# Spreading the Fourier transform of u over more steps of an attention loop

## The chip, the cores and the metric

The kernel runs on one core of a Trainium2 chip. The metric is the device time of one execution in microseconds, as the median of several runs. A core has five engines with a queue each: TensorE (PE, with its weight loads shown as PEld), VectorE (DVE), ScalarE (ACT), GpSimd (POOL) and SyncE (SP), which here issues all transfers between memory and the core.

## The reference

Two independent heads, whose outputs stand side by side. A is a long convolution from a state-space model: a kernel K of 2048 positions for each of 448 channels, made from 256 complex modes, is convolved with u by Fourier transforms. B is attention with 16 heads of 28 channels over 2048 positions.

```
# A: L = 2048, D = 448, N = 256
P = exp((A * dt[:, None])[:, :, None] * pos)
K = 2.0 * einsum("dn,dnl->dl", C, P).real
y = irfft(rfft(u_t, 2 * L) * rfft(K, 2 * L))[:, :, :L]
a = y.transpose(0, 2, 1) + u * D_skip
# B: H = 16, Dh = 28
q, k, v = split(x @ wqkv)
p = softmax(q @ k.T * Dh ** -0.5)
b = (p @ v).reshape(B, S, D) @ wo
out = concatenate([a, b], axis=-1)
```

## The kernel before

The program has a first part, a loop of 256 steps, and an end. All of it is written out in Python, and each engine gets its instructions in the order in which they were issued there.

The first part projects x to q, k and v, and makes the seeds of the convolution kernel, which it stores in memory. The loop does the attention: step s works on query block s // 16 (four groups of four heads, and four blocks of 512 queries in each) and on the 16th part s % 16 of the keys. While the loop runs, head A's work is done in between, by four sorts of tasks:

- *u tasks*: the transform of u. `u_stage1` has 16 jobs and `u_stage2` 16 more, of two parts each, so 64 tasks. A part does one product with a transform matrix (`mm32`, in four pieces of 32 rows, each of which the profile shows as two matmuls, so eight records), and ScalarE copies the result to a tile ub (two copies in stage 2). After the second part the result is stored, and the loads of the job after the next are issued. Inputs come in tiles ua, of which there are two.
- *k tasks*: the 56 blocks of the convolution kernel. A block begins every `KP` = 3.5 steps (`k_begin`). GpSimd then raises the powers of its e tile with nine operations (`e_power`: three sizes, three operations each), VectorE those of its g tile, and `KD` = 4 steps later PE multiplies them in three tasks, one a step: two products of e and g (`part0`), and a transform (`part1`). A block's e tile can be seeded when the products of the block before the last have been issued (`k_seed`).
- tasks at the end of a query block: `sums`, `scale` and the turning of the maxima, three in 16 steps.
- from step 192 on, the products of the spectra, the transform back, and the output (`f_slot`).

The order within a step is written out by hand in `ORDER`. For PE it is: two pairs of score products (one for the running maximum of a later block, tile pm, one for the probabilities, tile pss), a first slot, the product of probabilities and v (`pv_step`, tile po), a second slot, and two more pairs. A slot takes at most one task, in the order of `slot`: urgent ones first, then a k task that is due, then a u task that is due. The results of max products and of all tasks go through one ring of three PSUM tiles, pm.

```
ORDER = ('m0', 's0', 'm1', 's1', 'v', 'f', 'pv', 'f', 'v', 'k', 'm2', 's2', 'm3', 's3', 'v')
...
u_due = collections.deque((3 + UP * i + (UP / 2) * c + (4 if i > 15 else 0), i, c) for i in range(32) for c in range(2))
...
        elif m_due and m_due[0][0] <= s_:
            m_due.popleft()[1]()
        elif u_due and u_due[0][0] <= s_:
            u_part(*u_due.popleft()[1:])
```

After the very last u task, `load_wo` takes both ua tiles for the weights of the output projection: GpSimd clears each, and SP issues eight loads into each.

Of the kernel before, what the change touches and what calls it, by code (L numbers as in the profile page):

```python
# [39 lines left out]
UG = (2, 2, 4)  # L40
PS = 1
SGB, XB, XL = 2, 5, 4
K0, KP, KD, UP = 0, 3.5, 4, 3
A0, A1, KW = 26, 34, (33, 35, 36)

N1 = 32
# [1083 lines left out]
```

## Time and profile before

| | |
|---|---|
| median of 3 runs | 1302.44 us (1301.22 to 1304.79) |
| span of the profiled execution, first to last instruction | 1301.1 us |
| mean clock granted to TensorE in it | 0.978 |
| starts of the loop's first and last exponential | 254.7 and 1276.4 us |

The profiled execution's time is given as its span alone; no other time of it is on the page. The page gives the busy time of each engine over the span, the chain of waits that ended last, the costliest groups of instructions and the transfers; the trace behind it can be asked for any stretch. Where a row of a timeline ends in brackets, the engine sat idle before it for that time, until what stands behind the arrow was done. Nearly all instructions are recorded through one helper, so they show its line, 75, and are told apart by their tiles: out<-in.

### The profile page before, as it was taken

What the parts mean: (1) busy time and instruction counts of PE and PEld (TensorE: products, weight loads), DVE (VectorE), ACT (ScalarE), POOL (GpSimd) and SP (SyncE); (2) the same over time, 40 slices, a digit from 0 to 9 for tenths busy, and PEclk for the clock granted to TensorE, in tenths of its full rate; (3) what the DMA queues carried; (4) which work ended last, traced back from release to release, by engine and by line L of the source; (5) the groups of instructions that cost most, each with busy time, mean ns of one, the idle gap of its engine ahead of it and who ended that gap; (6) DMA issues with size and microseconds to landing.
All of it is one profiled execution on the core that took longest, in us unless ns stands there. A gap on an engine that the chain in (4) does not pass through costs nothing.

```text
span 1301.1 us, 33177 instructions
## 1 busy us (share of the span) xinstructions
PE 1228.2 (94%) x12625; PEld 701.0 (54%) x12625; DVE 948.0 (73%) x2106; ACT 952.4 (73%) x2068; POOL 871.1 (67%) x736
## 2 busy tenths in 40 slices
PE   6878985899999999999999999999999999999997
PEld 5657763355555555555555555555555555544433
DVE  5887896987777887787788888888888655645111
ACT  4775763488888888888888888888887766756552
POOL 3676683298888878888869999998996212424421
PEclk9888997999999999999999999999999999999999
DMA  6677769835866555458644131733425453647656
GB/s 194 203 258 244 249 206 294 237 77 124 195 137 149 124 146 148 140 147 231 181 126 96 54 95 32 182 91 83 103 51 148 153 158 133 201 144 244 198 162 174
DMA packets 200088, 205.35 MB, mean 158 GB/s; under 512 B 95993, under 2 KB 158521, under 8 KB 197881
## 3 DMA queue, kind: packets, MB, share of 16 engines
q1 hardware_dynamic: 199928, 203.23, 56.2%
q8 instruction: 100, 1.64, 0.5%
q14 instruction: 60, 0.48, 0.1%
HBM read 120.73 MB, written 82.18 MB: 156 GB/s over the span
## 4 chain that ended last, share of the span: by engine, by line
PE 71%; DVE 10%; DMA 6%; POOL 5%; ACT 3%; issue 3%; SPq 0%; POOLq 0%; ACTq 0%; DVEq 0%
PE pm L75 40%; PE pss L75 16%; PE po L75 15%; DVE tri L75 2%; DVE mx L75 2%; POOL e L75 1%; POOL qhat L75 1%; DMA k<-hl 1%; ACT tri L75 1%; DVE qhat L75 1%; DVE sg L75 1%; DMA tri<-in_B_wqkv 1%; DVE px L75 1%; DMA khat<-k 1%; DMA ut<-in_A_u 1%
## 5 line engine op out<-in xcount | busy, mean ns | idle before, releaser
L75 ACT ACTIVATE p<-pss 128x512 f32<-128x512 f32 x1024 | 560.9, 609 | 111.6 <-PE pss L75 108.6
L75 PE MATMUL pss<-qhat,khat 128*128 128x512 f32 x1024 | 402.5, 399 | 1.5 <-ACT p L75 1.4
L75 DVE TENSOR_REDUCE mx<-pm 128x1 f32<-128x512 f32 x500 | 321.4, 684 | 109.2 <-PE pm L75 107.1
L75 PE MATMUL pm<-khat,qhat 128*128 128x512 f32 x749 | 326.3, 438 | 3.4 <-DVE mx L75 2.1
L75 POOL TENSOR_TENSOR e<-e,sdb 128x256 f32<-128x256 f32 x168 | 202.0, 1202 | 116.2 <-ACT e L75 61.2
L75 PE MATMUL po<-p,v 128*32 128x512 f32 x2048 | 269.1, 594 | 0.0
L75 POOL TENSOR_TENSOR e<-e,eu 128x256 f32<-128x256 f32 x168 | 248.4, 1478 | 13.2
L75 PEld LDWEIGHTS pm<-khat,qhat 128*128 128x128 f32 x749 | 141.0, 189 | 199.7 <-ACT p L75 47.8
L75 DVE CUSTOM_DVE_ANT_0 rl<-pm,rl 128x512 f32<-128x512 f32 x249 | 171.4, 688 | 65.2 <-ACT rl L75 61.5
L75 PEld LDWEIGHTS pss<-qhat,khat 128*128 128x128 f32 x1024 | 190.2, 188 | 45.7 <-issue 10.8
L75 POOL TENSOR_TENSOR eu<-e,sdb 128x256 f32<-128x256 f32 x168 | 202.2, 1203 | 0.0
L75 POOL TENSOR_TENSOR p<-pr,pr 64x448 f32<-64x448 f32 x64 | 73.3, 1145 | 158.5 <-PE pm L75 133.2
L75 ACT ACTIVATE rl<-pm 128x512 f32<-128x512 f32 x249 | 150.8, 606 | 20.4 <-PE pm L75 20.4
L75 DVE TENSOR_TENSOR g<-g,zg 128x128 f32<-128x128 f32 x392 | 162.1, 413 | 3.4
L75 PE MATMUL pm<-xh,khat 112*128 112x512 f32 x256 | 94.1, 451 | 23.2 <-DVE hl L75 11.1
L75 PE MATMUL pm<-kdif,qhat 128*128 128x512 f32 x249 | 100.5, 404 | 2.6 <-DMA v<-v 1.3
L75 DVE TENSOR_TENSOR zg<-g,zg 128x128 f32<-128x128 f32 x224 | 88.0, 393 | 5.0
L75 PEld LDWEIGHTS pm<-e,g 128*32 128x32 f32 x3584 | 57.2, 109 | 43.8 <-issue 16.1
L75 DVE TENSOR_TENSOR pr<-pm,ub 128x448 f32<-128x448 f32 x64 | 37.0, 619 | 56.4 <-PE pm L75 42.0
L75 PEld LDWEIGHTS pm<-xh,khat 112*128 112x128 f32 x256 | 54.2, 217 | 39.4 <-DVE hl L75 12.9
L75 PE MATMUL pm<-e,g 128*32 128x64 f32 x3584 | 73.0, 222 | 1.9 <-POOL e L75 1.9
L75 ACT ACTIVATE y<-pm 128x448 f32<-128x448 f32 x48 | 26.5, 553 | 58.2 <-PE pm L75 33.8
(134 smaller groups left out, 1470.3 us busy)
## 6 DMA issues: line engine op xcount, KB each, us to landing
sdb<-sd SPq DMA_DIRECT2D x56, 336.0 KB
khat<-k SPq DMA_DIRECT2D x64, 256.0 KB
qhat<-q SPq DMA_DIRECT2D x64, 256.0 KB
sd<-sg SPq DMA_DIRECT2D x8, 1456.0 KB
k<-hl SPq DMA_DIRECT2D x16, 512.0 KB
q<-hl SPq DMA_DIRECT2D x16, 512.0 KB
mw<-in_mw SPq DMA_DIRECT2D x16, 512.0 KB
sd<-qhat SPq DMA_DIRECT2D x8, 896.0 KB
```

The lines of the kernel that those rows point to most:

```text
L75: i = f(*args, **kw)
```

## The change

One constant, the distance in steps from one job of the transform of u to the next. Task c of job i was due at step 3 + 3i + 1.5c and is now due at 3 + 5.5i + 2.75c, with four steps more from job 16 on in both. The last task fell in step 102 and now falls in step 181. The clearing of the ua tiles and the loads in `load_wo` move with it.

```diff
 PS = 1
 SGB, XB, XL = 2, 5, 4
-K0, KP, KD, UP = 0, 3.5, 4, 3
+K0, KP, KD, UP = 0, 3.5, 4, 5.5
 A0, A1, KW = 26, 34, (33, 35, 36)
```

## The prediction

> **What bounds the kernel now.** I read the page's table of engines first, then the busy time of each engine in stretches that hold whole steps of the loop, then the chain of waits inside a few steps, then GpSimd's timeline around the end of the transform of u.
>
> ```profile
> PE 1228.2 (94%) x12625; PEld 701.0 (54%) x12625; DVE 948.0 (73%) x2106; ACT 952.4 (73%) x2068; POOL 871.1 (67%) x736
> ```
>
> TensorE is the busiest by far, but its busy time alone doesn't say that it is the limit, so the two stages that the change touches are set side by side: the steps that carry u tasks and the steps after them that carry none. The first view counts the matmuls of `pv_step` (tile p, eight records in every step), the second the u tasks (tile ua, eight records a task), the third is of all instructions.
>
> ```profile
> core 0: us, PE busy (x) PEld busy (x) ACT busy (x), PEclk, DMA share, GB/s
> 264.30:666.30 402.00, 104.45 (x800) 20.69 (x796) 3.84 (x6) 1.00 0.60 150
> 692.90:981.10 288.20, 84.93 (x648) 16.28 (x648) 3.16 (x5) 1.00 0.37 87
> ...
> 264.30:666.30 402.00, 59.41 (x508) 15.73 (x504) 1.70 (x2) 1.00 0.60 150
> 692.90:981.10 288.20, 0.00 (x0) 0.00 (x0) 0.00 (x0) 1.00 0.37 87
> ...
> 264.30:666.30 402.00, 400.49 (x4782) 219.27 (x4778) 313.36 (x742) 335.73 (x778) 326.08 (x257) 1.00 0.60 150
> 692.90:981.10 288.20, 287.16 (x3461) 163.72 (x3453) 253.00 (x607) 244.18 (x553) 271.19 (x212) 1.00 0.37 87
> ```
>
> The first stretch is 800 / 8 = 100 steps in 402.0 us, 4.02 us a step, with 508 / 8 = 63.5 u tasks in it (the 64th lies across its edge). The second is 648 / 8 = 81 steps in 288.2 us, 3.56 us a step, without any. So the stage with the tasks pays (4.02 - 3.56) x 100 / 63.5 = 0.73 us for each. In the last two rows the columns after the length are PE, PEld, DVE, ACT and POOL. PE is busy for 99.6% in both. Beside it POOL is at 81% and 94%, DVE at 78% and 88%, ACT at 84% and 85%: the second stage is much nearer to even, and whether PE still sets its pace is the question on which the sign hangs. The chain of waits inside steps answers it. These are three neighbouring steps of the first stage:
>
> ```profile
> 604.90 0.58 PE pm L75 x32
> 605.48 0.86 PE po L75 x8
> 606.34 1.18 PE pm L75 x9
> 607.52 0.23 PE pss L75
> ...
> 609.15 0.58 PE pm L75 x32
> 609.74 0.86 PE po L75 x8
> 610.60 0.43 PE pm L75
> ...
> 613.23 0.86 PE po L75 x8
> 614.09 1.19 PE pm L75 x9
> ...
> 616.92 0.89 PE pm L75 x8
> 617.81 0.86 PE po L75 x8
> 618.67 0.43 PE pm L75
> ```
>
> A step reads: a k task in the first slot (0.58), the four `pv` products (0.86), whatever the second slot holds together with the first score product (0.43 with nothing, 1.18 with a u task), and seven more score products at 0.23. With a k task alone that is 0.58 + 0.86 + 0.43 + 7 x 0.23 = 3.48 us, and the rows agree: 609.74 to 613.23 is 3.49. With a u task as well it is 3.48 + 0.75 = 4.23; 605.48 to 609.74 is 4.26. And this is a stretch from the stage without u tasks:
>
> ```profile
> 843.12 0.86 PE po L75 x8
> ...
> 846.59 0.86 PE po L75 x8
> 847.45 0.43 PE pm L75
> ...
> 849.50 0.99 PE po L75 x8
> 850.50 0.43 PE pm L75
> ...
> 852.71 0.60 PE pm L75 x32
> 853.30 0.86 PE po L75 x8
> ```
>
> 843.12 to 846.59 is 3.47: a step with a k task takes there what it takes among u tasks, PE issuing without a break. Only the step with nothing in its slots (its `pv` starts at 849.50) is another matter: from 846.59 to 849.50 PE needs 2.91 us, and the next step, to 853.30, takes 3.80, some 0.3 us more than its work, since others fall behind there. The two steps together take 6.71, so an empty one is worth 6.71 - 3.48 = 3.23, not the 2.91 that PE needs.
>
> [...] The steps' own times, equal to the sum of PE's issue times, speak for PE.
>
> **The change part by part.** The due time of task c of job i goes from 3 + 3i + 1.5c to 3 + 5.5i + 2.75c (both with 4 more from job 16 on). The last goes from 101.5, which is step 102, to 180.25, step 181. No work is added or removed: the same 64 tasks of eight matmuls, 96 evacuations by ScalarE and the same loads and stores, in the same order among themselves. Kernel blocks keep their steps, as a k task comes before a u task in `slot`. By the due times 28 of the 64 tasks go past step 104.
>
> *Where a task lands.* Blocks start every 3.5 steps and have three k tasks each, so six of seven steps hold one. A task in such a step costs 0.75 in either stage, by the rows above. A u task in an otherwise empty step takes the first slot (0.89 at 616.92): 613.23 to 617.81 is 4.58, of which 0.75 is the task ahead of it at 614.09, so such a step takes 3.83, 0.60 more than an empty one. Going through `slot` with both sets of due times, 51 of 64 tasks share a step with a k task now, and 52 afterwards; three steps hold two u tasks and no k task now, none later. That is 1 x (0.75 - 0.60) = 0.15, and the pairs cost 0.75 for one of their two at most: I take **+0.2 us**, between -2 and +2 if the cost differs by 0.03 a task between stages.
>
> *GpSimd's wait for the last task.* `load_wo` clears the two ua buffers on POOL, behind which the powers of e wait in POOL's queue; the second clearing waits for the last u task on PE.
>
> ```profile
> 649.49 2.39 POOL L75 TENSOR_TENSOR e<-e,eu 128x1024 f32<-128x1024 f32 x1
> 652.25 0.85 POOL L75 MEMSET ua<- 128x896 f32 x1 [0.38 <-PE pm L75]
> 664.24 0.85 POOL L75 MEMSET ua<- 128x896 f32 x1 [11.14 <-PE pm L75]
> 665.05 0.63 POOL L75 TENSOR_TENSOR e<-e,sdb 128x256 f32<-128x256 f32 x1
> ...
> 670.71 1.92 POOL L75 TENSOR_TENSOR e<-e,sdb 128x1024 f32<-128x1024 f32 x1
> ...
> 674.58 2.38 POOL L75 TENSOR_TENSOR e<-e,eu 128x1024 f32<-128x1024 f32 x1
> 676.91 0.64 POOL L75 TENSOR_TENSOR e<-e,sdb 128x256 f32<-128x256 f32 x1
> ...
> 688.75 0.63 POOL L75 TENSOR_TENSOR e<-e,sdb 128x256 f32<-128x256 f32 x1
> ...
> 677.01 0.65 PE L75 MATMUL pm<-e,g 128*32 128x64 f32 x32 [0.63 <-POOL e L75]
> ...
> 688.84 0.65 PE L75 MATMUL pm<-e,g 128*32 128x64 f32 x32 [1.27 <-POOL e L75]
> ```
>
> POOL loses 11.14 us of its lead, and PE then waits 0.63 + 1.27 = 1.9 us for the next two blocks. This stall moves to step 181 and changes its shape. In the built program the clearing now stands between the sixth and the seventh of the nine operations of block 51, whose products are due in step 183; before, it stood ahead of all nine of block 29, with four steps to go. After the release POOL needs 0.81 for the clearing and 676.96 - 670.71 = 6.25 for the three large operations: block 51 is ready 7.1 us on. PE gets there in the rest of step 181 with the start of 182 (eight score products, 2.0) and step 182, which has no k task (about 3.2): 5.2. It waits 1.9. Block 52 needs a whole period, 688.75 - 676.91 = 11.84, so 18.9 us on; PE, at 7.1 plus three steps of 3.48, is there at 17.5 and waits 1.4. Block 53 is due four steps later, 13.9 against 11.84: no wait. In all 3.3 in place of 1.9, **+1.4 us**, between -1.9 (POOL far enough ahead) and +7 (below).
>
> *What is hidden.* The 16 loads of wo stand in SP's queue behind the clearing, ahead of loads of seeds for block 54 and of v for the last head group, all due five or more steps later. ScalarE's evacuations and the u loads and stores (DMA share 0.60 in the first stage, 0.37 in the second) go from the fuller to the emptier stage; no row above has PE waiting for either, so their move is worth nothing, and costs nothing as long as ACT, 85% in the second stage, stays under PE: a task costs ACT (335.73 / 100 - 244.18 / 81) x 100 / 63.5 = 0.54 us, less than the 0.75 by which it lengthens the step.
>
> Sum: 0.2 + 1.4 = +1.6 us. On the profiled execution's span of 1301.1 that gives 1302.7. The median of the runs is 1302.44, 1.3 above that span, and the forecast on it is **1304.0 us**.
>
> **The rivals.** *The second stage has room (faster).* If POOL, DVE or ACT set the pace there, PE has slack into which 28 tasks fall for less than 0.75, while the first sheds them at full price. By PE's issue times seven steps need 6 x 3.48 + 2.91 = 23.8, or 3.40 a step, against 3.56 measured, part of which are the tasks at the end of a query block. If all 0.16 over 76 steps were filled, 12 us would go: about 1292. For it speak POOL's 94% and the 0.3 us lost after an empty step; against it that the k step takes 3.47 to 3.49 in both stages, so there is nothing to fill in six steps of seven. [...]
>
> *POOL arrives late at step 181 (slower).* If POOL has not done the first six operations of block 51 when the last u task ends, they come after it. They take 670.71 - 665.05 = 5.7 us, the first wait grows to 7.5 and the second stays: 9 us in place of 1.9, with the 0.2 about 1309.7. By `k_seed` the seeds of block 51 can be written in step 177, four steps or some 14 us ahead of the release, and six operations fill 5.7 of these; it decides when POOL comes to them more than 8 us late. For it speaks POOL's 94% in the second stage, against it that with u tasks in it a block's 3.5 steps take some 13 us of PE against POOL's 11.84.
>
> *The loads of wo come in the way (slower).* If the 16 issues push a load of seeds past its use, a wait like the 1.27 above comes with each of the two to four blocks still to go: 1307 to 1309.
>
> **How the numbers follow.** About 0.3% (3.9 us) is what a measurement of this kernel can tell from no change. The forecast has 0.61, the room in the second stage 0.15, the late POOL 0.16, the loads of wo 0.08. The forecast lies within 0.3% over its own range of 1300 to 1306. The range reaches half way to the first rival, of which it leaves the rest out, and to the end of the two slower ones: 1297.0 to 1310.0. Faster by over 0.3%: 0.15; within: 0.61; slower: 0.24.
>
> **What would show it.** In the changed profile steps with a k task alone should still take 3.48 us and those with a u task 4.25, in the old second stage too; that stage, which gets 26 tasks, should grow from 3.56 to about 3.80 a step, and the first, which keeps 35, fall to about 3.81. GpSimd's wait before its second clearing should stand near step 181, with PE's two waits of 1 to 2 us for e behind it, and none near 677. Steps of the second stage that take less than 4.1 us with both tasks would prove the first rival; a wait for e over 5 us the second; waits of PE or ACT for sdb after step 181 the third.

## The result

The changed kernel takes 1308.26 us in the median of 7 runs (1306.13 to 1312.1), the kernel before 1303.8 over the 7 runs that stand beside it; the ratio is 1.0041 with a 95% interval of 1.0026 to 1.0056, about 5.3 us (the medians differ by 4.5). The profiled execution of the changed kernel has a span of 1304.4 us (its own time 1306.55), 3.3 more than before. The loop itself differs by more than that: from the first exponential to the first one of step 192 it takes 734.9 us against 729.9 before (worked out from the starts of the exponentials, four in a step). The part ahead of the loop, which is the same program, ended 2.2 us earlier in this profile; over all profiles of this study it ended between 252.5 and 257.0 us, so spans are not compared below, but the loop.

Busy time in the two stages of the prediction, 100 and 81 steps, first by the products with v (eight records a step), then for all engines (PE, PEld, DVE, ACT, POOL after the length):

```profile
261.60:644.40 382.80, 104.60 (x800) 20.58 (x800) 3.88 (x6) 1.00 0.50 120
670.10:983.70 313.60, 84.90 (x648) 16.76 (x648) 3.13 (x5) 1.00 0.48 126
```

```profile
261.60:644.40 382.80, 380.04 (x4559) 211.59 (x4555) 312.63 (x743) 319.40 (x723) 332.41 (x262) 1.00 0.50 120
670.10:983.70 313.60, 307.86 (x3677) 171.58 (x3677) 254.98 (x607) 260.36 (x608) 262.81 (x209) 1.00 0.48 126
```

The first stage falls from 4.02 to 3.83 us a step, where 3.81 was forecast. The second rises from 3.56 to 3.87, where 3.80 was forecast, and PE, busy for 99.6% of it before, is at 98.2%: it waits there for things for which it did not wait before. The waits of PE and its weight loads in the loop up to step 192, those that are new or larger (engine and tile, what it waited for, us in total, times, longest):

```profile
PEld pm L75 <- issue: 49.1, 139, 1.7
PEld pm L75 <- POOL e L75: 6.7, 10, 2.2
PE pm L75 <- POOL e L75: 3.2, 2, 1.9
PEld pss L75 <- DMA qhat<-mh: 1.6, 1, 1.6
PE pm L75 <- issue: 1.6, 1, 1.6
PE pss L75 <- DMA qhat<-mh: 1.2, 1, 1.2
```

The same rows in the list of the kernel before:

```profile
PEld pm L75 <- issue: 46.7, 140, 0.8
PEld pm L75 <- POOL e L75: 5.1, 9, 1.7
PE pm L75 <- POOL e L75: 1.9, 2, 1.3
```

Three things stand here. The wait for e was forecast; it takes 3.2 us of PE in place of 1.9. The waits of PE for the store of the maxima (qhat<-mh) and for nothing that the profile shows (issue) have no row in the kernel before. Comparing each step's length with the mean of steps of the same kind (same tasks in its slots, same neighbour) in the kernel before, the long steps are 31 and 32 (+1.5 us together), 114 (+1.9), 183 (+2.0) and 186 (+1.3) in the changed kernel, and 106 (+0.7) and 109 (+1.3) in the one before. That is 6.7 against 2.0, so 4.7 of the 5.0 us. The steps with a task of u behave as forecast: in the old second stage of the changed kernel the 18 steps with a k task and a u task take 4.25 us in the median, from one product with v to the next.

*The wait for e.* GpSimd's and TensorE's timelines around step 181:

```profile
937.41 0.84 POOL L75 MEMSET ua<- 128x896 f32 x1
947.22 0.85 POOL L75 MEMSET ua<- 128x896 f32 x1 [8.97 <-PE pm L75]
948.03 1.91 POOL L75 TENSOR_TENSOR e<-e,sdb 128x1024 f32<-128x1024 f32 x1
...
954.31 0.65 PE L75 MATMUL pm<-e,g 128*32 128x64 f32 x32 [1.90 <-POOL e L75]
957.82 0.65 PE L75 MATMUL pm<-e,g 128*32 128x64 f32 x32
966.15 0.65 PE L75 MATMUL pm<-e,g 128*32 128x64 f32 x32 [1.28 <-POOL e L75]
```

POOL had reached its first clearing at 937.41, ten microseconds ahead of the release, and PE then waits 1.90 and 1.28 us for blocks 51 and 52.

*The maxima.* The first score product of step 32, the first of query block 2, waits for the store of that block's maxima into qhat. VectorE (the first row, which makes the first of the two halves that are stored), SP's queue (start, length) and PE in the changed kernel:

```profile
361.57 0.28 DVE L75 TENSOR_SCALAR mh<-pm 16x128 fp32r<-16x128 f32 x1
...
357.81 1.84 SPq L75 DMA_DIRECT2D yu_d<-ub  x4
359.75 1.86 SPq L75 DMA_DIRECT2D ua<-in_A_u  x4
361.71 1.71 SPq L75 DMA_DIRECT2D sdb<-sd  x1
363.46 1.82 SPq L75 DMA_DIRECT2D khat<-k  x4
365.38 1.23 SPq L75 DMA_DIRECT2D qhat<-mh  x2
...
372.18 0.47 PE L75 MATMUL pss<-qhat,khat 128*128 128x512 f32 x1 [1.23 <-DMA qhat<-mh]
```

The eight transfers of a u task, a load of seeds and four loads of khat stand right ahead of the store. The first half of the maxima is ready at 361.85, but SP issues its store only at 365.38, 3.5 us later; it lands near 372, when the last row, on PE, can start. In the kernel before:

```profile
369.10 0.28 DVE L75 TENSOR_SCALAR mh<-pm 16x128 fp32r<-16x128 f32 x1
...
358.53 1.85 SPq L75 DMA_DIRECT2D yu_d<-ub  x4
...
364.82 1.82 SPq L75 DMA_DIRECT2D khat<-k  x4
369.41 1.23 SPq L75 DMA_DIRECT2D qhat<-mh  x2
```

There the transfers of a u task stand ahead of the store too, but far enough: the loads of khat are issued by 366.64, and SP issues the store at 369.41, 0.03 us after the half is ready. The next task comes in step 30, behind the store.

*A pause inside a product.* In step 114, 27 matmuls of a k task run, then nothing for 1.58 us, then the other five; no wait on any engine or transfer is recorded for it:

```profile
687.18 0.61 PE L75 MATMUL pm<-e,g 128*32 128x64 f32 x27
689.37 0.31 PE L75 MATMUL pm<-e,g 128*32 128x64 f32 x5 [1.58 <-issue]
```

```profile
676.00:680.50 4.50, 4.50 (x28) 2.24 (x28) 3.85 (x10) 4.23 (x12) 4.34 (x4) 1.00 0.86 217
680.50:684.00 3.50, 3.50 (x81) 2.27 (x80) 3.23 (x11) 3.10 (x8) 3.42 (x3) 1.00 0.89 200
```

```profile
q8 instruction: 1, 0.02, 4.1%
```

The second fence is the busy time of the engines in two stretches ahead: the DMA engines are busy for 0.86 and 0.89 (the column before the last) while the 1 MB of qhat is loaded that SP issues from 678.21 on, and then for 0.61 up to the pause. The third, of the DMA queues between 686 and 688, shows a packet of the instruction queue there; it starts at 686.72 and takes 1.31 us, so it ends 1.34 us before PE goes on. The same product in the kernel before has no pause:

```profile
708.23 0.63 PE L75 MATMUL pm<-e,g 128*32 128x64 f32 x32
```

There SP issues the four loads of qhat from 699.75 on, the DMA engines are busy for 0.90 and 0.97 from 700.0 to 704.0 and to 708.2, and a packet of the instruction queue runs from 707.36 for 1.32 us.

### The profile page after: what moved, and what is told of

It reads as the page before. It is cut to its first block, busy times and chain, and to the rows that moved or that the text cites. A ratio compares the mean times of both kernels' runs of the same rounds, so it can differ in the third digit from the quotient of the medians.

```text
span 1304.4 us, 33179 instructions
## 1 busy us (share of the span) xinstructions
PE 1227.2 (94%) x12625; PEld 699.3 (54%) x12625; DVE 948.6 (73%) x2106; ACT 952.1 (73%) x2068; POOL 869.8 (67%) x736
## 4 chain that ended last, share of the span: by engine, by line
PE 75%; DVE 10%; DMA 4%; POOL 4%; ACT 4%; issue 2%; SPq 0%; ACTq 0%; DVEq 0%; POOLq 0%
PE pm L75 42%; PE pss L75 17%; PE po L75 16%; DVE mx L75 2%; DVE tri L75 2%; POOL qhat L75 1%; ACT tri L75 1%; DVE sg L75 1%; DVE qhat L75 1%; DVE px L75 1%; DVE rl L75 1%; DMA qhat<-q 1%; DMA k<-hl 1%; POOL tri L75 1%; DVE hl L75 1%
```

## The experiments

Times are compared with runs of the kernel before on the same chip. "Loop" is the time from the first exponential to step 192, as above.

| | ratio to before, 95% interval | loop, us |
|---|---|---|
| before (profile) | 1 | 729.9 |
| changed (profile) | 1.0041, 1.0026 to 1.0056 | 734.9 |
| e1 clearing on VectorE | 1.0008, 0.9999 to 1.0018 | 731.8 |
| e2 one u task two steps later | 1.0042, 1.0027 to 1.0056 | 732.8 |
| e3 qhat loaded four steps later | 1.0016, 1.0004 to 1.0028 | 732.3 |
| e4 all u tasks 75 steps later | 0.9997, 0.9985 to 1.0008 | 730.7 |
| e5 changed kernel again | 1.0042, 1.0026 to 1.0059 | 733.7 |
| e6 load_wo five steps later | 1.0013, 0.9999 to 1.0026 | 731.6 |
| e7 e6, e2 and e3 together | 0.9983, 0.9971 to 0.9995 | 728.6 |
| e8 before, load_wo five steps later | 0.9987, 0.9975 to 0.9998 | 728.3 |

**e1, the clearing on VectorE** (in the changed kernel)

```diff
-            nc.gpsimd.memset(t, 0.0)
+            nc.vector.memset(t, 0.0)
```

> The changed kernel, with the two clearings in load_wo done by VectorE in place of GpSimd. Theory (GpSimd's queue waits for the last u task, so the powers of e come late): the steps 183 and 186, 5.32 and 4.85 us in the changed kernel, go back to 3.4 and 3.5, 3.3 us less in the loop; VectorE follows TensorE closely, so its own wait delays nothing by more than 0.5 us. Against the kernel before about +2 to +3 us in place of +5.3. Rival (those two steps are long for another reason, such as the loads of wo on SP's queue): they stay long, time as the changed kernel.

Steps 183 and 186 are back at their usual lengths, so it was the clearing in GpSimd's queue. The ratio gives +1.0 us against the kernel before (-0.1 to +2.3), less than the 2 to 3 expected. VectorE paid a little, too:

```profile
950.61 1.75 DVE L75 MEMSET ua<- 128x896 f32 x2
...
953.32 0.50 PE L75 MATMUL pm<-khat,qhat 128*128 128x512 f32 x1 [0.69 <-DVE mx L75]
```

Its two clearings hold up a reduction of maxima, and PE waits 0.69 us for it, a little over the 0.5 allowed. The wait for the maxima (0.7) and the pause (1.9) are still there.

**e2, one task behind the store of the maxima** (in the changed kernel)

```diff
-    u_due = ... + (4 if i > 15 else 0), i, c) ...
+    u_due = ... + (4 if i > 15 else 0) + (2 if (i, c) == (4, 1) else 0), i, c) ...
```

> The changed kernel, with one u task, the second part of job 4, due in step 30 in place of 28, behind the store of the maxima for query block 2. Theory (its four stores and four loads stand ahead of that store in SP's queue, together with four loads of khat): the wait of the score products for qhat<-mh near 372 us goes, steps 31 and 32 take 4.5 and 3.5 together 1.5 us less, all else as in the changed kernel. Rival (the store is late by the loads of khat alone): the wait stays within 0.3 us of its 1.6.

The wait for qhat<-mh is gone from the list of waits, and steps 31 and 32 are of usual length. SP issues the store at 365.21, as the next thing behind the loads of khat, and the task's transfers only from 370.04 on: they had made it late. The total did not fall: the ratio, 1.0042, is that of the changed kernel. Of the loop's 2.2 us less than in the changed kernel, 1.5 are this wait, but in the profile something else had come: after the wait for e in step 183, 1.89 us against 1.90 in the changed kernel, the granted clock was 0.56 for 3.9 us. Busy time around it, clock in the third column from the end:

```profile
953.70:955.60 1.90, 0.04 (x1) 0.00 (x0) 1.80 (x7) 1.43 (x3) 1.90 (x2) 1.00 0.39 100
955.60:959.50 3.90, 3.87 (x44) 1.98 (x45) 0.67 (x2) 0.22 (x1) 3.74 (x5) 0.56 0.55 146
959.50:963.00 3.50, 3.50 (x50) 2.04 (x49) 3.06 (x8) 2.98 (x8) 3.34 (x3) 1.00 0.29 104
```

A mean of 0.56 over 3.9 us is as much as half the clock for (1 - 0.56) x 3.9 / 0.5 = 3.4 us. The eight records of the products with v took 1.96 us there and 1.04 in the next step. Step 183 takes 6.9 us here, against 5.3 in the changed kernel; step 186 is of usual length, since POOL, busy for 3.74 of the 3.9 us, caught up meanwhile, and the one wait of PE without a recorded cause is 0.5 us against 1.6. On time alone e2 is inconclusive.

**e3, qhat loaded later** (in the changed kernel)

```diff
-        if kt == 2:
+        if kt == 6:
             if u + 2 < NU:
                 load_q(u + 2)
```

> The changed kernel, with the loads of the query block after the next issued in the seventh step of a block in place of the third (steps 118, 134 and so on in place of 114, 130). Theory (the pause of 1.6 us inside a product of step 114 is TensorE out of instructions, whose fetch stood behind 1 MB of loads of qhat): no pause in step 114, which takes 4.3 in place of 6.3; 1.9 us less, unless another fetch falls behind the moved loads, then one such pause at another place. Rival (the pause belongs to that place in the program whatever is loaded): step 114 stays at 6.3.

Step 114 is of usual length, and no pause over 0.5 us stands anywhere else in the loop: the list of waits has no row of PE for issue. With these loads four steps later the pause does not come; the loads alone do not make it, as the kernel before has them at the same place and no pause. That it is TensorE's instructions that come late behind them was the author's estimate: no row shows the engine waiting for instructions, and whose instructions a packet holds is not shown. The change of the loop is 2.6 us, 1.9 of it this step; the rest is the wait for the maxima, shorter in this run.

**e4, all u tasks in the second stage** (in the kernel before)

```diff
-u_due = collections.deque((3 + UP * i + ...
+u_due = collections.deque((78 + UP * i + ...
```

> The kernel before (3 steps from job to job), with all due times 75 steps later: the u tasks lie in steps 78 to 179. Theory (a task costs 0.75 us wherever there is a k task in its step): steps 3 to 77 fall to about 3.55 on average, steps 103 to 179 rise to about 4.0, the sum within 1 us of before; GpSimd's wait as before, 1.9 us in all, near step 180; in all -1 to +3 us against before, the upper end if a fetch or a store comes late somewhere. Rival (the second stage has room beside TensorE): 64 tasks there cost clearly under 0.75, 8 us or more less than before.

The same steps, 3 to 77 and 104 to 180, of e4 (first the products with v, then its u tasks) and, in the third fence, of the kernel before:

```profile
264.60:531.00 266.40, 78.65 (x600) 14.98 (x600) 2.51 (x4) 1.00 0.35 82
636.70:946.60 309.90, 80.38 (x616) 16.15 (x616) 3.15 (x5) 1.00 0.58 151
```

```profile
636.70:946.60 309.90, 44.16 (x376) 11.45 (x376) 1.69 (x2) 1.00 0.58 151
```

```profile
264.00:564.00 300.00, 78.36 (x600) 15.57 (x600) 2.50 (x4) 1.00 0.56 136
669.70:946.30 276.60, 80.70 (x616) 15.47 (x616) 3.16 (x5) 1.00 0.38 91
```

The first 75 steps lose 33.6 us, the later 77 gain 33.3 for 376 / 8 = 47 tasks, 0.71 each. So in that stage, too, a task costs about what it costs in the first, and TensorE has no room there to take it in. A pause came here too: the list of waits has one of PE for issue, of 1.2 us, ahead of a score product (pss).

**e5, the changed kernel once more**

> The changed kernel itself once more, for a second profile and more runs beside the other kernels of this set. Theory: the same four terms: score products waiting for qhat<-mh in step 31 or 32 (0.5 to 1.5 us), TensorE without instructions for 0.5 to 2 us in step 114, the waits for e in steps 183 and 186 (3.3 us), now and then half the clock for 3.4 us after one of these waits (1.7 us more); ratio 1.003 to 1.005. If the first two are chance of one run, they are missing here.

The pause is there after the same 27 matmuls, with 1.59 us, steps 183 and 186 are the same to 0.02 us, and the wait for the maxima is 0.5 us in the weight loads alone. So the pause and the waits for e belong to the program, and the maxima come at the edge: the weight loads wait 0.5 to 1.6 us for them by the run (1.1, 1.0 and 1.1 in e1, e3 and e6), and in this run no step is long for it. The lists of e1 and e6 have a wait of PE for issue as well, of 1.9 and 2.1 us. Behind the wait for e in step 183, 1.89 us, the eight records of the products with v take 1.04 us in this run, not 1.96 as in e2.

**e6, load_wo five steps after the last u task** (in the changed kernel)

```diff
         if c and i == 31:
-            load_wo()
+            wo_wait.append(5)
+
+    wo_wait = []
...
+        if wo_wait:
+            wo_wait[0] -= 1
+            if not wo_wait[0]:
+                wo_wait.clear()
+                load_wo()
         late[0] = s + NK + LEAD > NS
```

> The changed kernel, with load_wo called five steps after the last u task, so that GpSimd finds the buffers free. Theory: no wait of GpSimd on TensorE, no wait for e in steps 183 and 186, no half clock there: 3.3 us less than the changed kernel in the loop and up to 1.7 more of the clock; VectorE has no part in it, so nothing as at step 182 in the run with VectorE. Ratio to before 1.000 to 1.001. Rival (the clearing itself or the loads of wo delay the powers): waits for e of over 1 us two to four steps after the moved call.

GpSimd clears both tiles in one go, and the products of blocks 51 to 54 find their powers ready:

```profile
956.71 1.64 POOL L75 MEMSET ua<- 128x896 f32 x2
...
953.47 0.66 PE L75 MATMUL pm<-e,g 128*32 128x64 f32 x32
956.97 0.65 PE L75 MATMUL pm<-e,g 128*32 128x64 f32 x32
963.96 0.65 PE L75 MATMUL pm<-e,g 128*32 128x64 f32 x32
967.44 0.65 PE L75 MATMUL pm<-e,g 128*32 128x64 f32 x32
```

Neither the clearing itself nor the loads of wo delay anything: the list of waits has no row of PE for e or for a load of seeds. The loop is 3.3 us shorter than in the changed kernel, though its pause was longer (2.1 us against 1.6). The ratio, 1.0013, is a little over the 1.000 to 1.001 expected, well within its interval.

**e7, all three edits** (e6, e2 and e3 in the changed kernel)

> The changed kernel with all three edits: load_wo five steps later, the second part of job 4 due two steps later, the loads of qhat four steps later. Theory (nothing else is in the change): no step from 4 to 191 is over 0.45 us longer than its kind, and the loop up to step 192 takes 728 to 729.5 us, against 729.9 in the kernel before and 734.9 in the changed one; ratio to before 0.9985 to 1.000. Rival (spreading costs by itself): the loop stays above 731 us with no single long step.

No step is over 0.45 us longer than its kind. The stages:

```profile
265.30:646.50 381.20, 104.62 (x800) 20.48 (x800) 3.83 (x6) 1.00 0.51 119
672.30:981.00 308.70, 84.78 (x648) 16.64 (x648) 3.13 (x5) 1.00 0.50 128
```

3.81 us a step in both, the values that the prediction gave for a change without stalls (3.81 and 3.80). The ratio, 0.9983, is just below the range expected. Spreading by itself costs nothing that can be measured.

**e8, load_wo later in the kernel before** (the edit of e6)

> The kernel before, with load_wo called five steps after the last u task. Theory: its waits for e in steps 106 and 109 go, 1.9 us less: ratio 0.998 to 0.9995. Rival (VectorE or ScalarE hold those steps anyway): no change in them.

The waits in steps 106 and 109 are gone, 1.6 us of the loop. Beside e7's 728.6 the 728.3 of this kernel shows what the spreading of tasks costs when nothing stalls: +0.3 us, from one profile of each, and with the two other edits of e7 in it. e7 and e8 are both faster than either kernel; they differ from each other by less than the intervals can tell.

## Why the prediction was right or wrong

*What bounds the loop, and where a task lands (+0.2 us).* Right. A task costs the same in both stages: 0.73 us on average in the first stage of the kernel before, 0.71 in the second stage in e4, and the steps with both kinds of task take the 4.25 us that were forecast. The term itself is +0.3 by e7 against e8, which single profiles can't tell from nothing.

*GpSimd's wait (+1.4 us).* Right in place, form and size. Forecast were waits of 1.9 and 1.4 us for blocks 51 and 52 and none for 53; measured 1.90 and 1.28 and none. In the kernel before the two were 0.63 and 1.27. e6 shows that this, and not the clearing or the loads, is the cause.

*What is hidden (0).* Wrong, and this is the step that failed. The prediction looked for rows of the kernel before in which PE waits for u's transfers, found none, and valued their new places at nothing. It had asked which loads stand behind the clearing on SP's queue, but not what each u task's eight transfers come to stand ahead of. Those of one of the 64 now stand, with four loads of khat, so close ahead of the store of the maxima that SP issues it 3.5 us after it could: the score products behind it wait 0.5 to 1.6 us (e5 and the changed kernel), and e2 takes the wait away.

*The pause in step 114 (1.9 us)* had no term at all. What brings it is not shown: the kernel before has none, though the same 1 MB of qhat is loaded ahead of the same product (DMA engines busy for 0.97 up to it, against 0.61 in the changed kernel), e4, with the tasks moved otherwise, has one of 1.2 us, and with the loads four steps later (e3, e7) there is none.

*The sum.* +1.6 was forecast, +5.3 measured, inside the range, and the interval of 0.26% to 0.56% lies mostly beyond the 0.3% within which the likeliest case put it. That the range covers it is luck: its slower end was set by the late POOL and the loads of wo, of which neither came, and what came instead was not in the sum. The forecast terms came out at 0.3 + 1.3, the two missing ones at 1.5 + 1.9: 5.0, as the loop of the profiled run shows. In e5 the wait for the maxima cost next to nothing (loop 733.7), so 1.5 is the most that was seen of it. The lower clock of e2 (0.56 for 3.9 us) can come on top; in the stretches of the loop that are shown of the kernel before, the changed kernel, e4 and e7 the granted clock was 1.00, and how often it falls is open.

*The rivals.* Room in the second stage: refuted by e4. POOL late at step 181: it was 10 us early, even more than the 8 us of lead that the prediction reckoned with. Loads of wo in the way: no wait of that kind in any run. The time went to the slower side by two waits that were not among the rivals: the one for the maxima is of the sort of the third, a transfer that comes late, and what the other waits for no row shows.

## What to carry to other kernels

TensorE bounds this loop in both stages (busy for 99.6% of each in the kernel before), so the moved work cost nothing that could be measured: of the 5.0 us in the loop, 1.3 and 1.5 came from what it newly stood next to, and 1.9 from a pause whose cause is not shown. When tasks are moved in such a loop, list, for each engine and above all for the queue that issues the transfers, what every moved item comes to stand ahead of, and look for short deadlines there. An instruction that waits for the last user of a buffer is better placed as many steps behind that user as its queue runs ahead; here five steps were worth 1.6 us of the loop before and 3.3 of the changed one, more than the placing of the tasks itself.

## What the runs showed of the hardware

TensorE stopped in the middle of a product, after 27 of 32 matmuls and without any recorded wait, for 1.58 and 1.59 us in two profiles of the changed kernel; e1 and e6 list one such stop each, of 1.9 and 2.1 us. With the loads of qhat issued four steps later (e3, e7) none is listed, and none in the kernel before, with the loads at the same place. What TensorE waited for, no run here shows.

Behind a wait of 1.89 us TensorE's granted clock was once 0.56 (e2, 955.6 to 959.5), while behind the same wait of 1.90 it was 1.00 in the changed kernel (953 to 957 and 957 to 961), as it was behind the pause of 1.58 us (689.4 to 693.4). What decides whether the clock falls after such a wait, no run here shows.
